# Where the first half of wo stands in a read queue: behind V of load 1 or behind V of load 4

## The chip, the core and the metric

The kernel runs on one core of one Trainium2 chip. The metric is the device time of one execution in microseconds, as the median of several runs. Beside it there is one profiled execution, whose trace gives every number of the text that isn't a run's time.

## What is computed

One decode step for 8 sequences: attention over the last 2048 positions of a cache, with 32 query heads on 8 key/value heads, and then a small mixer with a two-layer perceptron. With one token for each sequence, the mixer's shifted branch is zero. Cut to what matters:

```python
def _A_ref(x, k_cache, v_cache, wq, wo):
    # B = 8, Hq = 32, Hkv = 8, Dh = 128, Sk = 8192, W = 2048
    q = (x @ wq).reshape(B, 1, Hq, Dh).transpose(0, 2, 1, 3)
    k = repeat(k_cache[:, :, Sk - W:, :], 4, axis=1)
    v = repeat(v_cache[:, :, Sk - W:, :], 4, axis=1)
    p = softmax(einsum("bhqd,bhkd->bhqk", q, k) * Dh ** -0.5)
    o = einsum("bhqk,bhkd->bhqd", p, v)
    return o.transpose(0, 2, 1, 3).reshape(B, 1, Hq * Dh) @ wo

h  = x + _A_ref(layernorm(x), k_cache, v_cache, wq, wo)
y  = layernorm(h)
h2 = gelu(layernorm(y) @ w3) @ w4
out = h + y + h2
```

All inputs are bf16. The caches' windows are 32 MB each for K and V, wq and wo 4 MB each, w3 and w4 1.8 MB each: some 79 MB that have to be read once.

## The kernel before

**Loads.** The cache is read in 16 loads (NUN), two for each of the 8 sequences, each with four of the eight key/value heads. Load n has a K part, Kn, and a V part, Vn, of 2 MB each, read by `load_k(n)` and `load_v(n)`. One such DMA fills 128 partitions with 16 KB each, and it is spread over the core's 16 DMA engines, which each add one to the transfer's semaphore when their share has landed. A reader waits for all sixteen.

**Buffers.** K has four buffers in `knat`; the first four loads take one each, and loads 4 to 14 go alternately into the first two (`k_at`). So K5 waits until load 1's K has been turned, K6 until load 4's has, K7 until load 5's has. V has four buffers in `vnat`; loads 0 to 11 go alternately into the first two (`v_at`). So V2 waits until the PV matmuls of load 0 are done, V3 for those of load 1, and so on. wq and wo share the tile `wbig`: each half of wo overwrites half of wq, so `load_wo` waits for the matmuls that make q (`e_q`).

**Compute for a load.** TensorE (PE) turns K of a load in four blocks (`turn_K`, the matmuls of line 404, 24 of them in the first stretch of a load and 8 more behind its first QK), and ScalarE and VectorE evict them (lines 391 and 392). Then come the scores (`pe_QK`, line 419). After the second load of a sequence there is its softmax (`softmax_1` to `softmax_5`). The PV matmuls (`pe_PV`, line 536) run three loads behind the K side (LVD = 3): in the turn of load n, PE works on PV of load n - 3. The product with wo (`pe_wo`, line 626) comes at the very end, first for wo's first half and then for its second, and after it w3 (line 781) and w4 (line 815).

**The order of the reads.** All large reads are issued by SP's queue (SyncE), and SP issues them strictly in program order: where one has to wait for its buffer, all behind it wait too. The DMA engines take them in that order. ScalarE issues only the read of x; GpSimd (POOL) issues none. The order is written out by the main loop over n: K of load n, then V of load n - 3, and, in one turn of the loop, wo's first half:

```python
            if n < NUN - 1:
                load_k(n)
            if n == NUN - 2:
                load_k(n + 1)
            if n >= LVD:
                load_v(n - LVD)
            if n == WO_AT:
                load_wo(0, sem_wo)
```

With WO_AT = 7 the queue reads wq, K0, K1, K2, K3, V0, K4, V1, K5, V2, K6, V3, K7, V4, wo's first half, K8, V5, K9, V6 and so on. Behind the last loads come wo's second half, two parts of w3 and four of w4, which end the reads.

Of the kernel before, what the change touches and what calls it, by code (L numbers as in the profile page):

```python
# [36 lines left out]
NV = 4  # L37
NKT = 4
LVD = 3
WO_AT = 7  # L40
KR = 16
QR = 16 // R
QW = 24 + 32
# [121 lines left out]
def bass_sequential_preLN__sliding_block_cached__mixer_s_mlp__decode_kernel(  # L165
# [32 lines left out]
    with es:  # L198
# [400 lines left out]
        def load_v(n):  # L599
            b, t = divmod(n, NU)  # L600
            src = A_v_cache[b, J * t:J * (t + 1), W0:SK, :].rearrange("j (r c) d -> r j (c d)", r=RR)
            old = before(v_at, n)[0]
            dma(SP, vnat[:, v_at(n), :], src, sem_v[v_at(n)], None if old is None else e_PV[U * (old + 1) - 1])

        def load_wo(t, sem):
            dma(SP, wo_v[:, t, :, :].rearrange("p j n -> p (j n)"),
                A_wo[128 * KR * t:128 * KR * (t + 1), :].rearrange("(p j) n -> p (j n)", j=KR), sem, e_q)
# [56 lines left out]
        for n in range(NUN):  # L664
# [4 lines left out]
# [4 lines that stand above are left out]
# [193 lines left out]
```

## Time and profile before

| | |
|---|---|
| median of 3 runs | 195.18 us (195.14 to 195.6) |
| the profiled execution's own time | 195.46 us |
| its span, first to last instruction | 194.1 us |
| mean granted TensorE clock | 0.906 |
| read from HBM | 79.18 MB, 408 GB/s over the span |
| PE busy | 142.5 us (73% of the span) |
| VectorE (DVE) busy | 107.0 us (55%) |
| ScalarE (ACT) busy | 89.3 us (46%) |
| packets on the data queue | 5920, 96.7% of 16 engines' span |
| chain that ended last | DMA 51%, PE 31%, DVE 12% |

How to read the lines below: a time at the head of a line is microseconds from the span's start, then how long the group of instructions took, the engine, the line of the kernel, what is written from what, and how many instructions the group has. In square brackets stands the engine's idle time just ahead of the group, and what ended it. A line on SPq is the issue of a DMA, which takes SP about half a microsecond; the data lands later. In a table by windows each row is a stretch of time, with the busy time of each engine in it, the granted clock, the mean busy share of the 16 DMA engines, and GB/s. In the 40 slices of the page each slice is a fortieth of the span, 4.85 us.

### The profile page before, as it was taken

What the parts mean: (1) busy time and instruction counts of PE and PEld (TensorE: products, weight loads), DVE (VectorE), ACT (ScalarE), POOL (GpSimd) and SP (SyncE); (2) the same over time, 40 slices, a digit from 0 to 9 for tenths busy, and PEclk for the clock granted to TensorE, in tenths of its full rate; (3) what the DMA queues carried; (4) which work ended last, traced back from release to release, by engine and by line L of the source; (5) the groups of instructions that cost most, each with busy time, mean ns of one, the idle gap of its engine ahead of it and who ended that gap; (6) DMA issues with size and microseconds to landing.
All of it is one profiled execution on the core that took longest, in us unless ns stands there. A gap on an engine that the chain in (4) does not pass through costs nothing.

```text
span 194.1 us, 4605 instructions
## 1 busy us (share of the span) xinstructions
PE 142.5 (73%) x1972; PEld 111.5 (57%) x1972; DVE 107.0 (55%) x281; ACT 89.3 (46%) x115; POOL 7.0 (4%) x29
## 2 busy tenths in 40 slices
PE   0028985896899699734887795969887897797674
PEld 0027763664767477614766564847665574696572
DVE  4502454874677586720857492467674965843241
ACT  6000765853748284622646453528473664250041
POOL 4000001000000100010000100010001000000000
PEclk9999999999999999985999998799999999855555
DMA  6999999999999999999999999999999999999991
GB/s 218 432 419 429 429 432 429 432 432 432 390 372 415 432 432 431 429 429 429 432 429 429 429 426 426 422 431 426 432 429 429 429 429 432 426 426 416 406 375 37
DMA packets 5948, 79.36 MB, mean 409 GB/s; under 512 B 672, under 2 KB 688, under 8 KB 1456
## 3 DMA queue, kind: packets, MB, share of 16 engines
q1 hardware_dynamic: 5920, 79.18, 96.7%
q8 instruction: 9, 0.15, 0.3%
q10 hardware_dynamic: 16, 0.01, 0.0%
q14 instruction: 3, 0.02, 0.0%
HBM read 79.18 MB, written 0.01 MB: 408 GB/s over the span
## 4 chain that ended last, share of the span: by engine, by line
DMA 51%; PE 31%; DVE 12%; ACT 2%; SPq 2%; issue 2%; DVEq 0%
DMA knat<-in_A_k_cache_dram 39%; PE kT_ps L404 19%; DMA knat<-in_B_w_dram 12%; PE S_ps L419 5%; DVE kT_sb L392 5%; PE S_ps L473 3%; DVE Pz L466 3%; SPq L295 2%; ACT pS L483 2%; PE oT_ps L536 1%; DVE mcol L429 1%; PE sm L555 1%; DVE pS L488 1%; DVE Mrow L435 1%; PE sm L433 1%
## 5 line engine op out<-in xcount | busy, mean ns | idle before, releaser
L391 ACT ACTIVATE kT_sb<-kT_ps 128x1024 bf16<-128x1024 bf16 x64 | 62.6, 1023 | 38.9 <-PE kT_ps L404 38.8
L404 PE MATMUL kT_ps<-perm_k,knat 128*128 128x128 f32 x512 | 68.5, 288 | 9.1 <-DMA knat<-in_A_k_cache_dram 8.6
L404 PEld LDWEIGHTS kT_ps<-perm_k,knat 128*128 128x128 f32 x512 | 60.0, 148 | 17.1 <-DMA knat<-in_A_k_cache_dram 10.4
L392 DVE TENSOR_SCALAR kT_sb<-kT_ps 128x512 int32<-128x512 int32 x64 | 43.5, 688 | 41.3 <-PE kT_ps L404 41.3
L466 DVE TENSOR_TENSOR Pz<-P_sb,mJ 128x256 bf16<-128x256 bf16 x64 | 23.9, 417 | 0.0
L419 PE MATMUL S_ps<-kT_sb,qz 128*32 128x512 bf16 x256 | 19.9, 383 | 3.8 <-DVE kT_sb L392 3.4
L536 PE MATMUL oT_ps<-vnat,pS 128*32 128x256 bf16 x416 | 17.5, 275 | 4.5 <-DVE oM L583 3.7
L546 ACT ACTIVATE oE<-oT_ps 128x256 f32<-128x256 f32 x13 | 5.0, 384 | 32.3 <-PE oT_ps L536 32.3
L536 PEld LDWEIGHTS oT_ps<-vnat,pS 128*32 128x32 bf16 x416 | 9.2, 95 | 8.0 <-issue 5.3
L473 PE MATMUL S_ps<-perm_p,Pz 128*128 128x128 f32 x56 | 9.2, 286 | 1.7 <-ACT pS L483 1.7
L483 ACT ACTIVATE pS<-S_ps 128x1024 bf16<-128x1024 bf16 x7 | 7.2, 1024 | 6.6 <-PE S_ps L473 6.6
L376 POOL COPY qz<-q_sb 64x64 bf16<-64x64 bf16 x16 | 4.7, 291 | 140.4 <-PE S_ps L419 123.5
L473 PEld LDWEIGHTS S_ps<-perm_p,Pz 128*128 128x128 f32 x56 | 5.9, 140 | 6.3 <-ACT pS L483 3.3
L358 PE MATMUL S_ps<-xlnT,wbig 128*128 128x8 bf16 x128 | 3.6, 168 | 8.0 <-DMA wbig<-in_A_wq_dram 8.0
L429 DVE TENSOR_REDUCE mcol<-S_ps 128x1 f32<-128x512 f32 x8 | 5.5, 691 | 6.8 <-PE S_ps L419 6.8
L419 PEld LDWEIGHTS S_ps<-kT_sb,qz 128*32 128x32 bf16 x256 | 4.9, 95 | 6.4 <-ACT kT_sb L391 5.3
L358 PEld LDWEIGHTS S_ps<-xlnT,wbig 128*128 128x128 bf16 x128 | 3.5, 104 | 8.0 <-issue 8.0
L555 PEld LDWEIGHTS sm<-selo,oE 128*128 128x128 f32 x52 | 7.5, 208 | 0.4 <-ACT oE L546 0.4
L555 PE MATMUL sm<-selo,oE 128*128 128x16 f32 x52 | 7.4, 257 | 0.3 <-DVE negcol L448 0.3
L451 ACT ACTIVATE P_sb<-S_ps,negcol 128x512 bf16<-128x512 f32 x8 | 5.5, 687 | 4.2 <-DVE negcol L448 4.2
L567 DVE TENSOR_TENSOR oK<-o,mK 128x256 bf16<-128x256 f32 x16 | 6.8, 425 | 0.5
L787 ACT ACTIVATE Pz<-oT_ps,eps 128x8 f32<-128x8 f32 x1 | 0.3, 267 | 13.7 <-PE oT_ps L786 13.7
(100 smaller groups left out, 102.5 us busy)
## 6 DMA issues: line engine op xcount, KB each, us to landing
knat<-in_A_k_cache_dram SPq DMA_DIRECT2D x16, 2048.0 KB, 17.0
vnat<-in_A_v_cache_dram SPq DMA_DIRECT2D x16, 2048.0 KB, 18.3
wbig<-in_A_wq_dram SPq DMA_DIRECT2D x1, 4096.0 KB, 12.5
wbig<-in_A_wo_dram SPq DMA_DIRECT2D x2, 2048.0 KB, 17.8
knat<-in_B_w_dram SPq DMA_DIRECT2D x2, 896.0 KB, 19.9
knat<-in_B_w_dram SPq DMA_DIRECT2D x3, 512.0 KB, 21.9
knat<-in_B_w_dram SPq DMA_DIRECT2D x1, 256.0 KB, 22.8
x_sb<-in_A_x_dram ACTq DMA_DIRECT2D x1, 8.0 KB
```

The costliest lines, as they stand in the source:

```text
L358: ins = e.matmul(S_ps[0][:, h * B:(h + 1) * B], wq_v[:, kc, h * DH:(h + 1) * DH], xlnT[:, kc * B:(kc + 1) * B], start=(kc == 0), stop=(kc ...
L391: e_lo.append(AC.op(lambda e: e.activation(dst[:, 0:1024], ps[:, 0:1024], ACT.Copy), e_Tlo[k], *free))
L392: e_hi.append(DV.op(lambda e: e.tensor_single_scalar(dst[:, 1024:2048].bitcast(dt.int32), ps[:, 1024:2048].bitcast(dt.int32), 0, ALU.bitwi ...
L404: ins = e.matmul(ps[:, c * 128:(c + 1) * 128], src[:, c * 128:(c + 1) * 128], perm_k[:, :], is_transpose=True)
L419: ins = e.matmul(S_ps[0][32 * j:32 * (j + 1), :].rearrange("p (c r) -> p c r", c=16), qz[:, J * t + j, k, lo:lo + 32], kT[:, j, k], start= ...
L429: e_max[b] = DV.op(lambda e: e.tensor_reduce(mcol[:, :], S_ps[0][:, :], AX.X, ALU.max), e_QK[4 * b + 3], e_mT.get(b - 1), inc=3 if b == 1 ...
L466: e_Pz[b, part] = DV.op(lambda e, o=o, p_bc=p_bc, m_bc=m_bc: e.tensor_tensor(Pz[:, 0, J * o:J * (o + 64)].rearrange("p (x j k) -> p x j k" ...
L473: ins = e.matmul(ps[:, k * 128:(k + 1) * 128], src[:, c * 128:(c + 1) * 128], perm_p[:, :], is_transpose=True)
L483: e_pS[b] = (AC.op(lambda e: e.activation(pS[:, p_at(b), 0:1024], S_ps[1][:, :].bitcast(dt.bfloat16), ACT.Copy), e, p_free(b)),)
L536: ins = e.matmul(oT_ps[MO * q:MO * (q + 1), NO * (n % 2):NO * (n % 2 + 1)], pS[:, p_at(b), o:o + 2 * MO - 1:2], vnat[:, v_at(n), (16 * w + ...
L555: ins = e.matmul(sm[:, 32:48], oE[:, o:o + 128], selo[:, 16 * s:16 * s + 16], start=(s == 0), stop=(s == 2 * VP - 1))
L567: e_sc[n] = DV.op(lambda e: e.tensor_tensor(oK[:, n % 2], h_bc, k_bc, ALU.mult), e, e_mK, e_turn.get(n - 2))
```

## The change

One constant. wo's first half is issued in the turn of load 4 instead of that of load 7:

```diff
-WO_AT = 7
+WO_AT = 4
```

The queue then reads wq, K0, K1, K2, K3, V0, K4, V1, wo's first half, K5, V2, K6, V3, K7, V4, K8, V5 and so on. No instruction on another engine is added, removed or moved, and no buffer changes.

## The prediction

> **What bounds the kernel.** I read the page's slices first. DMA works at 9 tenths or more from the second slice to the last but one, at about 430 GB/s, except around the eleventh to thirteenth slice.
>
> ```profile
> span 194.1 us, 4605 instructions
> ...
> DMA  6999999999999999999999999999999999999991
> GB/s 218 432 419 429 429 432 429 432 432 432 390 372 415 432 432 431 429 429 429 432 429 429 429 426 426 422 431 426 432 429 429 429 429 432 426 426 416 406 375 37
> ...
> q8 instruction: 9, 0.15, 0.3%
> ```
>
> PE is busy 73% of the span and the other engines less, so the kernel is bound by its reads, and only a stretch in which DMA runs below its rate can be won. The windows of five microseconds place it (the last two columns are DMA share and GB/s):
>
> ```profile
> 45.00:50.00 5.00, 2.87 (x48) 1.79 (x49) 2.67 (x6) 1.48 (x3) 0.58 (x2) 1.00 1.01 429
> 50.00:55.00 5.00, 4.78 (x44) 3.85 (x42) 3.92 (x11) 4.06 (x6) 0.00 (x0) 1.00 0.99 392
> 55.00:60.00 5.00, 4.84 (x72) 3.96 (x72) 3.75 (x11) 2.97 (x5) 0.00 (x0) 1.00 0.98 374
> 60.00:65.00 5.00, 4.03 (x57) 2.96 (x59) 3.14 (x8) 2.69 (x3) 0.00 (x0) 1.00 1.00 423
> 65.00:70.00 5.00, 3.97 (x49) 2.99 (x38) 2.88 (x8) 2.93 (x6) 0.59 (x2) 1.00 1.01 433
> ```
>
> Against 429 the three middle rows lack 37, 55 and 6 GB/s for 5 us each: 490/429 = 1.14 us of the whole DMA side.
>
> The timeline of SP's queue shows why. In order these are V1, K5, V2, K6, V3, K7, V4, wo's first half, K8 (Kn and Vn are the K and V of load n):
>
> ```profile
> 24.69 0.60 SPq L295 DMA_DIRECT2D vnat<-in_A_v_cache_dram  x1
> 30.02 0.53 SPq L295 DMA_DIRECT2D knat<-in_A_k_cache_dram  x1
> 49.34 0.54 SPq L295 DMA_DIRECT2D vnat<-in_A_v_cache_dram  x1
> 54.89 0.54 SPq L295 DMA_DIRECT2D knat<-in_A_k_cache_dram  x1
> 57.32 0.53 SPq L295 DMA_DIRECT2D vnat<-in_A_v_cache_dram  x1
> 62.45 0.54 SPq L295 DMA_DIRECT2D knat<-in_A_k_cache_dram  x1
> 66.70 0.54 SPq L295 DMA_DIRECT2D vnat<-in_A_v_cache_dram  x1
> 67.28 0.59 SPq L295 DMA_DIRECT2D wbig<-in_A_wo_dram  x1
> 72.25 0.54 SPq L295 DMA_DIRECT2D knat<-in_A_k_cache_dram  x1
> ```
>
> Between 30.02 and 49.34 SP issues nothing: V2 waits until PV of load 0 has freed its buffer, and K6 then waits for the turning of load 4. The trace also records, for each transfer, when each of the 16 DMA engines reported its share landed. First and last of the sixteen, in us from the span's start:
>
> ```
> K0 17.39 18.14 | K1 22.29 24.31 | V1 46.75 48.87 | K5 51.65 53.78
> V2 56.66 58.82 | K6 62.45 65.25 | V3 67.34 70.15 | K7 72.24 75.05
> wo first half 82.02 84.84 | K8 86.92 89.73 | V6 first 101.60
> V14 first 170.10 | V15 174.99 177.81 | last of w4 188.71 191.46
> ```
>
> Two things stand in it. A queued transfer of 2 MB takes each engine 4.89 us (K6 to V3 to K7 to K8, first and last alike). And the engines are skewed: from K6 on one of them is 2.8 us behind the first, always. A reader of the buffer waits for that one, and so does the end: the last piece of w4 lands there at 191.46, the other fifteen are done by 190.67, and PE's last matmuls, two copies and the store make the rest of 194.1.
>
> What made the skew is the instruction queue, nine packets in the page. 0.3% of 16 engines' span is 0.003 x 16 x 194.1 = 9.3 us, 1.0 us for each. The packet records show 16 KB of instructions at 18.74 and 1.01 us long, and the data packet behind it takes 1.08 instead of 0.61: one engine lost 1.48 us there, and K1's last landing is 6.17 after K0's, 1.28 more than 4.89. A second such packet, at 60.28, fits K6's last landing.
>
> The Trainium skill, "Runtime: NRT & Kernel Launch", section on instruction fetch mechanics, says that instructions are refilled in 16 KiB blocks and that crossing one is mostly hidden. The block size agrees with the records; here it isn't hidden, for a data engine gave 1.48 us to it. By the skill's rule the whole skew would be starvation, and the change would win more (rival A).
>
> **The change, part by part.** *The issue.* One DMA of 2 MB, 0.59 us of SP, leaves the place after V4 (67.28) and comes behind V1, at about 25.2. SP then waits for K5's buffer until 30.02 anyway, which hides it; without this cover K5's issue would be 0.6 late, and it would still lie 21 us ahead of its transfer. The transfer itself waits on the q matmuls alone, which end at 17.0 by the timeline: satisfied at both places, and nothing is queued behind a new wait. At the old place SP waits for 72.25 in any case: nothing won. POOL issues no transfer, and its queue isn't passed. No instruction of PE, DVE, ACT or POOL changes; wo's first half is first read at 176.97 and lands near 53.8 instead of 84.84. Sum of issue: 0.
>
> *What is late.* K5, V2, K6, V3, K7 and V4 each stand 4.89 us further back. Where PE starts on a load:
>
> ```profile
> 57.20 2.86 PE L404 MATMUL kT_ps<-perm_k,knat 128*128 128x128 f32 x24
> ...
> 67.15 3.14 PE L404 MATMUL kT_ps<-perm_k,knat 128*128 128x128 f32 x24
> ...
> 75.09 2.87 PE L404 MATMUL kT_ps<-perm_k,knat 128*128 128x128 f32 x24 [0.46 <-DMA knat<-in_A_k_cache_dram]
> ...
> 89.78 4.34 PE L404 MATMUL kT_ps<-perm_k,knat 128*128 128x128 f32 x24 [4.66 <-DMA knat<-in_A_k_cache_dram]
> ```
>
> Loads 5 and 6 did not wait for their K. Now K5's last share lands at 53.78 + 4.89 = 58.7, so load 5 starts 1.5 late; K6's at about 69.8 (load 6: 2.7 late); K7's at about 79.6 (4.5 late). K8 stands where it stood in the order, so it lands at 89.4 to 89.7. PE took 10.0 us from 75.09 to its last work before that wait (4.66 before 89.78, so 85.1): from 79.6 it is ready at 89.6. The idle 4.66 us before load 8 becomes waits before loads 5 to 7, and by load 9 PE is where it was. Cost on the path: 0, hidden by that idle time; uncovered it would be the 1.5 us of load 5's start.
>
> *What SP issues late.* K7 follows load 5's turning: 62.45 + 1.5 = 63.9. The engine that is first then has V3 until 46.75 + 5 x 4.89 = 71.2, a margin of 7.3. K8 at about 75.0 has 6.0, K9 (80.35 + 4.5) has 5.9, K10 (about 96, against V6's first landing of 101.60 less the 1.0 that this engine wins) 4.6. The trace says what margin is enough: V2 (2.3 before 51.65) and K6 (1.8 before 56.66) lost time, V3 (5.1 before 62.45) none. For the engine that ends last add 2.8. No new gap there.
>
> *What is won.* V2 is now issued 7.2 us, and K6 6.5 us, before the first engine runs dry, so the gap closes. Its worth has two ends. Upper: 1.14 us, if all engines lost it alike. Lower: what the engine that ends last lost. Its two steps from K5 to K6 took 65.25 - 53.78 = 11.47, less 2 x 4.89 = 1.69, less one instruction packet at 1.28 to 1.48: 0.2 to 0.4 us (0.5 if it was the 53.66 of K5). The first engine's step to K6 was 5.78, 0.9 over, but that engine waits at the end anyhow. Below nothing the change itself has no term: the bytes are the same. I take 0.35, by the row of the engine that ends last. The span of 194.1, in an execution of 195.46, becomes about 193.75; from the median of 195.18, which lies 0.28 under that execution, **194.8**. Its own range is 194.6 to 195.2.
>
> **The rivals.** *A, the whole gap counts*: the 1.14 us of the windows come off, 194.0. For it: the GB/s row, and that skew may be different without the profiler. Against it: the last landings. The Trainium skill, "DMA: Bandwidth & Descriptors", section on the anatomy of one DMA, gives about 2.0 us fixed per transfer, beside bytes over 436 GB/s. By that page, as an estimate, two uncovered boundaries would be worth 4 us, 191.2. The record disagrees: the steps into V2 and K6 were 0.1 and 0.9 over 4.89 for the first engine, and the rule was fitted on another issue path.
>
> *B, an instruction packet leaves the last engine*: the second one (60.28) goes to another engine, since load 5 is shifted. Then the engine second to last at the end counts, 191.46 - 190.67 = 0.8, with the gap 1.15: 194.0. Against it: the engine was hit twice in the same way, which looks assigned.
>
> *C, the other side: one packet more on that engine.* Place: any of the five from 165.32 to 191.00, none of which moved the last landing (4.89 each from V13 to V15). From the point where one falls on the engine that is last, it costs 1.28 to 1.48: 195.18 - 0.35 + 1.4 = 196.2. For it: the requests follow the engines' progress, which shifts. Against it: after load 9 nothing shifts but 0.35.
>
> *D, PE's lateness reaches the end*: load 5's 1.5 us is kept, 196.6. PE's clock was 0.5 for some 7 us after the idle stretch at 85; a new wait of some 2 us before load 7 could slow it in the same way, 4.34 - 2.87 = 1.5 us per load. It decides once K10's issue is over 4.6 + 2.8 us later than I have it. For it: K10 is the thinnest margin. Against it: load 9 waited for its K even after the slow load 8. The Trainium skill, "TensorE: Matmul & The Clock Gate", part on the HAM clock gate, speaks for this rival: after an idle window of about 3.4 us, free-running, the clock is halved; 4.66 us idle here agrees, and 2 us may or may not.
>
> That the transfer doesn't move is excluded: SP issues in program order and its wait is met.
>
> **How the numbers follow.** Forecast 0.41, A 0.25, B 0.14, C 0.13, D 0.07. A measurement of this kernel tells about 0.3% from no change, 0.59 us, so 194.6 to 195.8 is no change. Faster is A + B = 0.39, no change the forecast's 0.41, slower C + D = 0.20. The range takes in A and B below and leaves out C and D: 193.8 to 196.0.
>
> **What would show it.** V2 and K6 land on all engines 4.89 after the transfer before (K6's last one later by an instruction packet); the windows from 50 to 65 move 429; load 5 starts at 58.7 behind DMA, load 7 at 79.6, load 8 near 89.5 with little idle before it; skew at the end still 2.8. A last landing of w4 near 191.1 is the forecast, near 190.3 is A or B (B if skew shrinks), over 192 is C or D (C if skew is 4.2, D if windows after 95 lie under 420). The forecast is wrong if the skew changes, or if SP's later issues leave an engine dry.

## The result and the profile after

The changed kernel takes 193.93 us (median of 11 runs, 193.62 to 195.38) where the kernel before takes 195.6 (median of 11, 194.38 to 196.45; its first three runs had given 195.18). The ratio is 0.9921, 95% interval 0.9895 to 0.9947: 1.5 us less (1.0 to 2.1), where 0.35 was predicted. A second set of runs of the same kernel gave 0.9913 (0.9878 to 0.9947). The predicted 194.8 lies in the right direction, but the predicted gain is too small by a factor of four. The profiled execution took 193.76 us; its page:

```profile
span 192.3 us, 4605 instructions
...
DMA  6999999999999999999999999999999999999991
GB/s 220 436 433 429 429 436 429 419 429 423 424 429 429 429 429 414 433 426 433 433 429 426 419 433 429 429 431 429 423 426 426 433 429 433 426 419 423 409 395 73
```

The eleventh and twelfth slices, 390 and 372 before, now have 424 and 429. The table by windows of the changed kernel (last column GB/s) shows the same, where 392, 374 and 423 stood:

```profile
50.00:55.00 5.00, 4.83 (x44) 3.90 (x43) 3.92 (x11) 4.01 (x6) 0.00 (x0) 1.00 1.03 431
55.00:60.00 5.00, 3.58 (x59) 2.68 (x60) 2.47 (x8) 1.69 (x3) 0.00 (x0) 1.00 1.01 429
60.00:65.00 5.00, 4.55 (x45) 3.54 (x43) 3.72 (x9) 4.01 (x5) 0.00 (x0) 1.00 0.99 419
```

The gap is closed. SP's queue after, in order V1, wo's first half, K5, V2, K6, V3, K7, V4, K8:

```profile
24.74 0.61 SPq L295 DMA_DIRECT2D vnat<-in_A_v_cache_dram  x1
25.39 0.59 SPq L295 DMA_DIRECT2D wbig<-in_A_wo_dram  x1
30.08 0.54 SPq L295 DMA_DIRECT2D knat<-in_A_k_cache_dram  x1
49.39 0.54 SPq L295 DMA_DIRECT2D vnat<-in_A_v_cache_dram  x1
54.94 0.54 SPq L295 DMA_DIRECT2D knat<-in_A_k_cache_dram  x1
57.37 0.53 SPq L295 DMA_DIRECT2D vnat<-in_A_v_cache_dram  x1
63.79 0.54 SPq L295 DMA_DIRECT2D knat<-in_A_k_cache_dram  x1
68.03 0.53 SPq L295 DMA_DIRECT2D vnat<-in_A_v_cache_dram  x1
73.58 0.54 SPq L295 DMA_DIRECT2D knat<-in_A_k_cache_dram  x1
```

V2 and K6 are issued at the same times as before, 49.4 and 54.9, but now there is work behind them in the queue. PE's first matmuls of loads 5 to 9:

```profile
58.53 2.87 PE L404 MATMUL kT_ps<-perm_k,knat 128*128 128x128 f32 x24 [1.21 <-DMA knat<-in_A_k_cache_dram]
...
68.48 3.14 PE L404 MATMUL kT_ps<-perm_k,knat 128*128 128x128 f32 x24
...
78.09 2.86 PE L404 MATMUL kT_ps<-perm_k,knat 128*128 128x128 f32 x24 [2.12 <-DMA knat<-in_A_k_cache_dram]
...
88.04 3.14 PE L404 MATMUL kT_ps<-perm_k,knat 128*128 128x128 f32 x24
...
97.66 2.54 PE L404 MATMUL kT_ps<-perm_k,knat 128*128 128x128 f32 x21 [2.15 <-DMA knat<-in_A_k_cache_dram]
```

The one idle stretch of 4.66 us before load 8 has become waits of 1.21, 2.12 and 2.15 us before loads 5, 7 and 9, and load 8 starts without one.

The landing events, as they were read in the prediction (us from the span's start; the mean is that of the sixteen engines):

```
                  first   mean    last
V2       before   56.66   57.47   58.82      after   61.41   62.05   63.38
K6       before   62.45   63.06   65.25      after   66.30   66.94   68.26
V4       before   77.13   77.77   79.94      after   80.98   81.66   82.95
last w4  before  188.71  189.78  191.46      after  187.65  188.78  189.75
```

From V2 to K6 the last engine needed 6.42 us before, and 4.88 after. At the end the mean engine is 1.0 us earlier, the last one 1.7 us.

### The profile page after: what moved, and what is told of

Its sections match the earlier page's. It is cut to its first block, busy times and chain, and to the rows that moved or that the text cites. A ratio compares the mean times of both kernels' runs of the same rounds, so it can differ in the third digit from the quotient of the medians.

```text
span 192.3 us, 4605 instructions
## 1 busy us (share of the span) xinstructions
PE 140.2 (73%) x1972; PEld 108.9 (57%) x1972; DVE 106.9 (56%) x281; ACT 89.0 (46%) x115; POOL 7.0 (4%) x29
## 4 chain that ended last, share of the span: by engine, by line
DMA 64%; PE 25%; DVE 5%; SPq 2%; ACT 1%; issue 1%
DMA knat<-in_A_k_cache_dram 52%; PE kT_ps L404 17%; DMA knat<-in_B_w_dram 12%; PE S_ps L419 3%; PE S_ps L473 3%; DVE kT_sb L392 2%; SPq L295 2%; ACT pS L483 1%; DVE Pz L466 1%; PE sm L555 1%; DVE mcol L429 1%; PE oT_ps L536 1%; PE S_ps L815 1%; DVE pS L488 0%; ACT out_sb L824 0%
## 5 line engine op out<-in xcount | busy, mean ns | idle before, releaser
L404 PE MATMUL kT_ps<-perm_k,knat 128*128 128x128 f32 x512 | 67.7, 286 | 8.9 <-DMA knat<-in_A_k_cache_dram 8.3
L404 PEld LDWEIGHTS kT_ps<-perm_k,knat 128*128 128x128 f32 x512 | 59.1, 147 | 17.1 <-DMA knat<-in_A_k_cache_dram 10.2
L555 PE MATMUL sm<-selo,oE 128*128 128x16 f32 x52 | 6.9, 245 | 0.3 <-DVE negcol L448 0.3
L555 PEld LDWEIGHTS sm<-selo,oE 128*128 128x128 f32 x52 | 6.8, 191 | 0.4 <-ACT oE L546 0.4
```

Source lines behind the costliest of these rows:

```text
L404: ins = e.matmul(ps[:, c * 128:(c + 1) * 128], src[:, c * 128:(c + 1) * 128], perm_k[:, :], is_transpose=True)
L555: ins = e.matmul(sm[:, 32:48], oE[:, o:o + 128], selo[:, 16 * s:16 * s + 16], start=(s == 0), stop=(s == 2 * VP - 1))
```

## The experiments

In what follows, *mean* and *last* are the mean and the last of the sixteen landings, and *skew* is last less first. All ratios are against the kernel before in the same set of runs.

### Each kernel once more: e1 and e2

No edit. 

> The kernel before, once more and unchanged: ratio 1.000 within its interval. It tells whether the second early packet of instructions (at 60.28 in the profile shown) falls again on the DMA engine that is last. Last-engine theory (the end is set by the one engine that lands last, by its own lost time and by the instruction packets that fall on it): the last landing of w4 moves with the skew between first and last engine. If the placing is fixed, skew 2.8 us and last landing near 191.4 again; if it is by chance, a skew of 1.4 to 2.2 and a last landing near 190.3 can come. Whole-gap theory (the end moves with the mean rate of all engines): last landing 191.4 whatever the skew.

> The changed kernel, once more: ratio 0.992 against the kernel before. Steps into V2 and K6 4.89 us on the last engine again. Last-engine theory: skew 2.1 and last landing 189.8 if the placing of instruction packets is fixed for a kernel; if it is by chance, up to 1.4 more in some execution. Whole-gap theory: 189.8 to 190.2 whatever the skew.

The kernel before: ratio 1.000 (0.9968 to 1.0032), profiled execution 194.47 us. Its gap is there, but the skew is 1.82 at V4 instead of 2.81, the last landing of w4 190.55 instead of 191.46, the mean 189.44 instead of 189.78. So one program gives different skews. Data and instruction packets of an engine follow each other within some 15 ns in the packet records, so the engine that got the packet at 60.3 can be followed to its landing. In both executions it became the engine that lands K6 last (65.25 and 64.00).

In the first of the two it can also be followed back. The sixteen landings of each transfer are:

```
V2   56.66 56.67 56.76 56.84 56.86 56.92 57.00 57.01 57.08 57.09 57.69 58.01 58.68 58.68 58.72 58.82
K6   62.45 62.46 62.47 62.48 62.49 62.60 62.68 62.74 62.81 62.81 62.94 63.61 63.71 63.75 63.79 65.25
```

The engine with the packet landed V2 at 58.01, as twelfth and 0.8 ahead of the last. Its next packet took 1.42 us instead of 0.61, which used up that lead, and then came the packet of instructions. The four engines behind it at V2 need at least 4.89 more, so they land K6 at 63.57 or later, and theirs are the landings from 63.61 to 63.79: they lost at most 0.2 us. In e4, below, the same happened to an engine of the front ten, whose next packet took 2.05 us.

The changed kernel: ratio 0.9913, last landing 189.89, mean 188.85, skew 2.23; steps into V2 and K6 4.89. Following the packet at 59.71 in its first profile, that engine lands V2 at 62.98, when the last one lands at 63.38: the packet cost the end nothing. The 12 runs of e1 lie between 194.23 and 196.54, and the 7 of e2 between 193.66 and 193.98.

### wo's first half at two other places: e3 and e4

```diff
-WO_AT = 7
+WO_AT = 5      # e3; 6 in e4
```

> wo's first half behind V2 instead of V1. V2 is still issued only 2.3 us before the first engine has finished K5 (gap at 51 to 53 stays), and only the gap at 56 to 59 (K6) is filled. Last-engine theory: the last engine lost some 0.1 to 0.2 us at the first gap, so nearly the whole gain stays: ratio 0.992 to 0.995. Whole-gap theory: by the windows 50:55 lost 0.43 us and 55:65 lost 0.71, so it wins 0.7 us: ratio 0.996.

> wo's first half behind V3. It comes after both gaps, so neither is filled, though it is read earlier than before and another load starts late. Both theories: windows 50:60 lack some 1.1 us as before, ratio 0.999 to 1.001. If the ratio is near 0.992 all the same, the gain has another source than the gap (PE's waits moved ahead, the clock, or where the instruction packets fall).

e3: ratio 0.9963 (0.993 to 0.9997). The step into V2 has a mean of 5.35 (0.46 over 4.89), that into K6 4.88. The expectation of the whole-gap theory was 0.996; of the last-engine theory 0.992 to 0.995; the interval holds both. e4: 1.0031 (0.9999 to 1.0064), no gain; the mean step into K6 was 6.26, and its last one 6.63, though K6 was issued 2.3 us before the first engine was dry, earlier than in the kernel before (1.8). wo's read being earlier is worth nothing when it stands behind the gap.

### A gap put into the changed kernel: e5 and e6

```diff
-  None if old is None else e_T[U * (old + 1) - 1])
+  None if old is None else e_T[U * (old + 1) + 0] if n == 10 else e_T[U * (old + 1) - 1])   # + 2 in e6
```

> The changed kernel with a gap put in elsewhere: K10 waits for the first turned block of load 9 (about 98.7) instead of the last of load 8 (93.1), so it is issued some 1.9 us before the first DMA engine is dry, as K6 was in the kernel before. First runs: the kernel before repeated has another skew (1.8 and 2.8), so packets of instructions fall on other engines in each execution. New theory (lead): front engines lead the last by 2 us, and a packet of 1.4 us that falls on one of them costs the end nothing; a gap eats this lead, and later packets then push the end. Lead: step into K10 first +0.6 to 1.0, last +0.1 to 0.9, skew falls below 1.7, and packets after it (128, 163, 171, 178, 185) push the last engine by 0.3 to 1.0 more; last landing of w4 190.2 to 191.3, ratio 0.994 to 0.999. Last-engine theory with nothing behind it: last landing 189.8 to 190.2, ratio 0.992 to 0.994. Whole-gap theory: mean step + 0.5 to 1.0 and the end the same amount later, 190.3 to 190.9, whatever the skew.

> The same gap, wider: K10 waits for the third block of load 9 (about 100.6), when the first engine is dry and the last has 1.9 us of V6 left; its packets start about 1 us later. Step into K10: first about +1.6 and more, last +0.1 to 0.9, skew under 1. Lead theory: packets after it hit engines without a lead; last landing of w4 190.8 to 192.0. Last-engine theory: 189.9 to 190.6. Whole-gap theory: mean step +1.2 to 1.8, end 191.0 to 191.7.

K10's issue and the window behind it, e5 first:

```profile
99.51 0.53 SPq L295 DMA_DIRECT2D knat<-in_A_k_cache_dram  x1
...
100.00:105.00 5.00, 4.76 (x40) 4.07 (x39) 3.14 (x8) 3.30 (x4) 0.00 (x0) 0.86 0.85 334
```

and e6:

```profile
102.58 0.53 SPq L295 DMA_DIRECT2D knat<-in_A_k_cache_dram  x1
...
100.00:105.00 5.00, 4.91 (x38) 4.21 (x36) 2.79 (x8) 2.98 (x4) 0.00 (x0) 0.79 0.34 118
```

```
step into K10    first   mean   last   skew after | last w4: mean    last   skew
e5                6.24   5.78   5.91      1.80    |        189.76  191.32   2.50
e6                8.92   8.47   7.24      0.65    |        192.36  193.58   1.89
(no gap, e2)      4.9    4.9    4.9       2.1     |        188.85  189.89   2.23
```

e5 bears most on the last-engine theory; its ratio alone does not decide, but its landings do. In e5 K10 was issued 0.9 us before the first engine was dry (100.41) and 3.0 us before the last one was (102.55), and no instruction packet is near. The last-engine theory gives the last engine next to nothing to lose, yet the last landing came 1.02 us late, as much as the mean (0.89). The sixteen landings show how:

```
V6   100.41 100.70 100.71 100.73 100.76 100.84 101.00 101.00 101.04 101.10 101.50 101.90 102.18 102.44 102.51 102.55
K10  106.65 106.67 106.68 106.69 106.72 106.75 106.76 106.77 106.79 106.80 107.29 107.43 107.51 107.66 108.16 108.46
```

The four late engines, with 4.89 more, would land K10 between 107.07 and 107.44, and four landings lie just 0.1 to 0.2 behind that. Two lie behind all of them, at 108.16 and 108.46. Followed from packet to packet, three of the four late engines land at 107.29, 107.43 and 107.51, the one that was last at V6 among them: those lost 0.2 us at most, as the theory has it. For the fourth and the last two landings the records leave open which is which, but at least one of the last two was an engine that had been ahead. So the last one isn't the same engine any more. When data came back, single packets of 16 KB took up to 1.14 us instead of 0.61, between 100 and 107. The mean is still 0.96 late at the end (189.76 against 188.80, the average of the kernels without a gap), and the last landing 1.6 (191.32 against 189.74). The ratio is 0.9943 (0.9909 to 0.9976): by the medians 0.6 to 0.8 us of the gain are given back (194.54 against 193.93 and, in its own set of runs, e7's 193.78). The profiled execution, 195.31 us, is one of the two longest of the twelve runs.

e6 was issued 2 us later than meant (102.58, since the third block of load 9 was turned later: its 24 matmuls took 4.51 us, at half clock), so its gap is wider than any theory was told. Of the mean loss of 3.57 the last landing lost 2.35 at once, and the skew fell to 0.65. By the end the skew was 1.89 again, and the last landing 3.8 later than without a gap (193.58 against 189.74): what the last landing did not lose in the gap, it lost afterwards. The records have four instruction packets of 16 KB in that stretch, from 167 to 189, and one of 8 KB at 129.9, and they fell on engines with little lead to spend. Ratio 1.0072 (1.0034 to 1.011).

### One place earlier, and the gap doubled: e7 and e8

```diff
-WO_AT = 7
+WO_AT = 3      # e7

+            if n == 5:             # e8, on the kernel before
+                load_v(n - LVD)
             if n < NUN - 1:
                 load_k(n)
...
-            if n >= LVD:
+            if n >= LVD and n != 5:
                 load_v(n - LVD)
```

> wo's first half behind V0, one place earlier still. The gap is filled as in the changed kernel, K4 comes 4.89 later as well (last share 48.7, against load 4's start at 49.8, so no new wait). All theories: steps into V2 and K6 4.89, last landing of w4 189.6 to 190.0, ratio 0.990 to 0.993.

> The kernel before with V2 issued ahead of K5: K5, free at 30, now waits behind V2 until 49.4, and all engines run dry after V1 (first 46.7, last 48.8). Data flows again at about 50.5. The step is then first +3.8, last +1.8 or a little more, skew near zero, and the packets at 50.4, 51.4 and 60 fall on engines without a lead (+1.4 on the last). K6 (54.9) is in time, so the second gap closes. Against the kernel before, whose last engine lost 0.8 to 1.7 between V1 and V3: last-engine theory without packets +0.5 to 1.0 us, ratio 1.003 to 1.005; lead theory 1.8 + 1.4 less 0.8 to 1.7, +1.5 to 2.4, ratio 1.008 to 1.012; whole-gap theory mean 3.6 less 1.1, +2.5, ratio 1.013.

e7: 0.9906 (0.9871 to 0.994), mean 188.77, last 189.59, skew 1.99: the same as the change. Both places ahead of the gap do.

e8: 1.0292 (1.0237 to 1.0347), 5.7 us, over all expectations. The first gap was as expected, 9.73, 9.38 and 7.91 for first, mean and last into V2, and skew 0.33. A packet then cost the last engine 1.32 in the next step. But load 5 came so late that K7 and V4 left a second gap, with mean steps of 5.71 and 6.02, which none of the theories had. From V1 to V4, six transfers, the mean took 35.88: 6.5 over 6 x 4.89. Less the gap of the kernel before, 1.0, that is 5.5, close to the 5.7 measured.

### Another read in the gap: e9 to e12

```diff
+            if n == 4:      # columns 0:8192 in e9, 0:4096 in e10, 0:2048 in e11 and e12
+                dma(SP, vnat[:, 3, 0:8192], A_wo[0:2048, :].rearrange(...)[:, 0:8192], sem_fill)
             if n == WO_AT:
                 load_wo(0, sem_wo)
```

on the kernel before, so WO_AT is 7; V13, the first to use this buffer, waits for it.

> The kernel before, with wo's first half where it was, and a further read of 2 MB behind V1, into a buffer that isn't in use then; nothing computes with it. It tells whether the gain is the cover of the gap or something in wo's new place. A read of 2 MB costs every engine 4.89 us. Cover theory (mean engine 1.0, and 0.6 more by skew): steps into V2 and K6 4.89, last landing of w4 189.74 + 4.89 = 194.6; against the kernel before + 4.89 - 1.55 = 3.3 us, ratio 1.017. If the gap isn't covered by it, +4.9, ratio 1.025.

> The same with 1 MB, 2.45 us an engine. V2 is then issued 2.3 + 2.45 = 4.7 us before the first engine is dry, and K6 1.8 + 2.45 = 4.2. If a margin of 4.2 is enough: steps into V2 and K6 4.89, ratio 1 + (2.45 - 1.55)/195.6 = 1.0046. If it needs the 5.1 at which V3 lost nothing, some part of the 1.0 us stays: up to 1.010.

> The same with 0.5 MB, 1.22 us an engine; margins 3.5 and 3.0. If 3.0 is enough: steps 4.89 and ratio 1 + (1.22 - 1.55)/195.6 = 0.998, a faster kernel that reads more. If the loss grows evenly from a margin of 5 down to 1.8, about half of the gap stays: 1.22 - 0.8, ratio 1.002.

> The half MB once more, since the first run left a question: its steps into V2 and K6 were 4.89 to 5.07 for the last engine, without a gap, yet its times (195.2 to 197.69) are as wide and as late as those of the kernel before. If the margin of 3.0 covers the gap in some executions alone: this profile shows mean steps into V2 or K6 over 5.1. If the first run's lateness was the placing of packets (skew 3.05 at V4): steps near 4.89 again, skew 2.0 to 2.4 and the last landing of w4 near 190.9, or a skew near 3 and 191.8 as in the first.

```
        read more   ratio (95%)                mean and last of w4   K6 ahead of a dry engine
e9      2 MB        1.0169 (1.0124, 1.0214)      193.72  194.75             4.0
e10     1 MB        1.0042 (1.0014, 1.0070)      191.31  192.42             4.3
e11     0.5 MB      1.0035 (1.0004, 1.0065)      190.22  191.86             3.0
e12     0.5 MB      1.0032 (0.9996, 1.0069)      190.49  192.58             2.9
```

The last column is the first landing of V2 less the issue of K6, in us. In e9 K6 was issued late, at 57.4: the first 24 matmuls of loads 0 and 2 took 5.38 and 4.25 us there, 4.30 and 3.14 in the kernel before. e9 and e10 came out as the cover theory said (1.017 and 1.0046). 2 MB more cost 3.3 us of the 4.89 that each engine works on them, 1 MB 0.8 of 2.45. It is the cover, and not wo's own place, that the change is worth. With half a MB the mean landing is 0.2 and 0.5 us later than a closed gap gives (190.22 and 190.49 against 188.80 + 1.22 = 190.02). In e11 this isn't the gap, since the steps into V2 and K6 are 4.90 and 4.98; in e12 the step into K6 has 0.3 of it. The skew at the end is 2.95 and 3.44. So 0.998 was wrong, while 1.002 lies in both intervals. In e11 the skew was made before the gap, by packets at 31.7 and 50.5 on engines that were late already; in e12 the step into K6 had a mean of 5.31, and a packet at 186.6 made its engine the last. Why chance was unkind in both executions, and in the median of both sets of runs, stays open.

## Why the prediction was right in its mechanism and wrong in its size

**What bounds the kernel, and the issue.** Right. SP issues V2 and K6 at the old times, nothing waits for the moved read, and the four engines' instructions are the same.

**What is late, and what hides it.** Right to some 0.2 us: load 5 starts at 58.53 (58.7 was said). Loads 6 to 8 start 1.3 to 1.5 us earlier than said, because the packet of instructions that had been left in K6's landing did not fall on the last engine (K6's last share lands at 68.26, not 69.8). K7 was issued at 63.79 (63.9), K8 at 73.58 (75.0), K10 at 93.13 (96).

**Rival D, PE's lateness and its clock.** Its trigger came true, its price did not. In the changed kernel's first profile, the waits of 1.21 and 2.12 us before loads 5 and 7 left the 24 matmuls at 2.87 and 2.86 us, where the wait of 4.66 had been followed by 4.34. But in e2, the same program, load 7 reads:

```profile
78.20 4.50 PE L404 MATMUL kT_ps<-perm_k,knat 128*128 128x128 f32 x24 [2.14 <-DMA knat<-in_A_k_cache_dram]
```

The granted clock was 0.5 there for 3.4 us, from 78.8, and e7 has the same at load 9. K9 was then issued at 85.10 instead of 83.34, still 5.7 us before the first engine was dry, and the execution took 193.95 us: the margin of the reads hid it.

**Rival C, a packet more on the last engine.** In the changed kernel's profile none of the five from 163.00 on moved the last landing. It can happen: in e12 the packet at 186.6 did, with a last step of 2.91 in w4's reads where the mean's was 1.82.

**What is won: the step that failed.** The prediction took as lower end "what the engine that ends last lost", took from it "one instruction packet at 1.28 to 1.48", and held of the first engine's 0.9 us that "that engine waits at the end anyhow". It chose 0.35. The range of 193.8 to 196.0 holds the result only because it took in rivals A and B; of the outcomes, no change (0.41) was put ahead of faster (0.39). Two things were wrong with the choice.

First, it took the last engine to be one and the same. Its 1.69 for two steps runs from the landing of one engine, 53.78, to that of another, 65.25: the engine hit at 60.28 had been twelfth at V2, with 58.01. That "the engine was hit twice in the same way" was a misreading too: the one hit at 18.74 landed K1 at 24.31, and with seven more transfers at 4.89 it can't land V2 before 58.54. The engine that is last loses little when the others run dry, but the others lose so unevenly that some fall behind it (e5: the last landing 1.02 late, the mean 0.89). What the end loses is near the mean loss. Three executions with the gap open (the kernel before twice, e4) have a mean landing of 189.83 on average, three with the gap closed (the change twice, e7) 188.80: 1.03 us, the 1.14 of the windows less a tenth. e3 (189.28 with 0.46 of the gap open), e9 and e10 (2 and 1 MB more) lie within 0.1 us of it.

Second, the instruction packet was treated as a cost of its own that the change doesn't touch. But whether it costs anything hangs on the gap. A packet that falls on a front engine is paid out of its lead of 2 us; after a gap that has eaten the lead, the same packet makes that engine the last. In the three executions with the gap open the last landing lies 1.55 behind the mean (191.38), in the three with it closed 0.94 (189.74): 0.6 us more, together 1.64, which is the measured 1.5 within its interval. Three executions a side are few, though: without e4, whose gap was the widest, the two parts are 0.8 and 0.5. That the skew comes back after a gap is shown by e6 (0.65 to 1.89), that the same packet is free on a front engine by the change's own profile.

The prediction's own test, a last landing near 190.3 with less skew for B, came nearest: 189.75, with 2.1. So rival A's sum (194.0) was right in amount, and of rival B the part that the second packet no longer makes its engine the last came true. B's reason, that load 5 is shifted, was wrong: where packets fall in the order of the engines varies between executions of one program (e11 and e12), and what the change alters is what they cost.

**The pages.** The Trainium skill, "Runtime: NRT & Kernel Launch", section on instruction fetch mechanics, calls the crossing of a block mostly hidden. The runs give the condition: with a full queue and a lead of 2 us it is (59.71 in the changed kernel), with the lead gone it costs about 1.4. The Trainium skill, "DMA: Bandwidth & Descriptors", section on the anatomy of one DMA, has 2.0 us fixed beside the bytes, 6.8 us for 2 MB as an estimate. e6, whose K10 met an empty queue on most engines, landed its first share 6.85 us after its issue (102.58 to 109.43): it agrees. So does e8, whose V2 met an empty queue on all of them, with 7.01 us (49.39 to 56.40). It holds for an empty queue. In the kernel before, the next transfer was issued some 2 us ahead, and the two boundaries cost a mean of 1.0 us, not 4.

## What to carry to other kernels

A kernel bound by its reads is as fast as its queue is deep at its thinnest point: look for the place where the next read is issued less than some margin, about 4 us in this kernel, before the first engine has the data ahead of it, and put a read there that waits for nothing. Count such a gap at the mean loss of all DMA engines, even if the engine that is last never ran dry, and add what the lost lead costs where a packet of instructions falls later. A transfer's last landing in one profile is a draw: judge by the mean of the sixteen.

## What the runs showed of the hardware

- With 2 MB reads queued at 4.89 us each, an issue 4.0 us before the first engine was dry cost nothing (e9), one of 2.9 to 3.0 us between nothing and 0.3 (e11, e12, mean step into K6 beyond an instruction packet's share), one of 0.9 us 0.9 (e5). The margin alone doesn't set the loss: K6 lost 0.6 us with 1.8 in the kernel before and 1.3 with 2.3 in e4, and V4 in e8 lost 1.1 with 2.75. What else does stays open.
- After a queue has nearly run dry, single 16 KB packets take up to 1.14 us instead of 0.61, for some 7 us (e5), 1.42 in the kernel before and 2.05 in e4, and the order of the engines changes.
- Where in the order of the DMA engines a packet of instructions falls differs between executions of one program: near 31.8 us it made the last landing of K3 0.45 us late in e11 and 0.03 in e12, with the same mean step (4.99 and 5.00).
- A wait of 2.14 us of TensorE was followed by 3.4 us at half clock in e2, one of 2.12 us by none in the first profile of the same kernel.
- With the gap closed the median and the fastest run lie within 0.3 us of each other (e2, e7, e9, e10); with it open, 1.0 to 1.5 us apart (the kernel before, e1, e4).
